# A filter layer and a feed-forward layer on one TensorE queue: stage 1 put well behind the transposing DMAs, groups placed anew, and the seven-product form from the third chunk on

## The chip, the cores and the metric

The kernel runs on one core of a Trainium2 chip. The time is the device time of one execution in microseconds (us). A profiled execution gives, beside its time, a trace of every instruction and DMA. Engines: PE is TensorE (PEld is its weight loading), DVE is VectorE, ACT is ScalarE, POOL is GpSimd, SP is SyncE, which here only starts DMAs. Each engine works through its own instructions in order.

## The reference

The reference filters a signal in the frequency domain and puts the result through a feed-forward layer:

```python
X = np.fft.rfft(x, axis=1)                      # x: 8 x 3008 x 256
y = np.fft.irfft(X * (filt_r + 1j * filt_i)[None], n=3008, axis=1)
h = y.reshape(24064, 256) @ w_in                # w_in: 256 x 2048
out = np.maximum(0.01 * h, h) @ w_out           # w_out: 2048 x 256
```

## The kernel before, in words

**The filter.** The FFT of 3008 = 94 x 32 points is done per batch entry in two steps, both as matmuls with constant matrices, then the multiplication, then the same two steps back. For batches 1 to 7 (batch 0 has a form of its own, at the head, from a list written out as text) there are four kinds of groups:

- stage 1 (`s1_group`, 16 groups per batch): four matmuls of 96 columns (L265) into one PSUM bank, and a copy (L266) by ScalarE, or by VectorE in some groups of batches 1 and 2, into the turn buffer `turn_in`.
- Six transposing DMAs (`t1_load`, L273) turn that buffer into six tiles `z1`. The buffer exists once: the copies of the next batch's stage 1 must wait until all six have read it.
- stage 2 (`s2_group`, 12 groups): two matmuls of 256 columns (L311); VectorE multiplies the bank with the filter (L320, L323); two DMAs exchange the halves of the partitions (L321, L322), except in every other group of batch 1, where VectorE writes the exchanged halves itself (L317, L318); GpSimd adds (L326).
- the first step back (`sa_group`): one matmul of 512 columns (L333), a ScalarE copy (L335), and after every second group a store to DRAM (L337). Eight loads (`t2_load`, L281) bring it back turned.
- the second step back (`sb_group`, 16 groups): four matmuls of 94 columns (L358) and copies (L347) into `yt`, the input of the feed-forward layer, a ring of six chunks.

**The feed-forward layer.** The 24064 rows go in 47 chunks of 512. For each chunk `moe1` does 32 matmuls of 512 columns (L524), and ScalarE takes each pair of results through the leaky ReLU (L527) into the chunk's tile. The second product is made one chunk later, in one of two forms:

- plain (`plain`): 4 x 16 matmuls of 256 columns (L689), a VectorE copy (L694) and a store for each of the four row tiles;
- seven products (`products`): seven products of 2 x 8 matmuls of 128 columns (L597), with four sums of activations made by VectorE ahead of them (`act_sums`, L563), one ScalarE copy (L637), and VectorE adds of the results (L625, L633, L641, L647, L650, L661). One of the seven is made a chunk later (`last_product`). Before the change chunks 0 to 2 are plain and chunks 3 to 46 have seven products (`W0 = 3`).

All results are stored through SyncE (L583), as are the transposing DMAs, the exchanges and the loads and stores of L281 and L337; loads of x go through GpSimd's queue (L204).

**The order.** Everything after the head is put in order by a planner that runs when the program is built. Its clock has 8 units for a chunk (some 15.3 us on the chip). Each chunk's matmuls have fixed places. Groups come from `PLANS`: for each batch the start and step of stage 1, start and step of stage 2, the lag of the first step back behind stage 2, start and step of the second step back, and start and step of the loads of x; batches above 4 repeat batch 4's row 47 units later. A group is taken at its time or at the first time at least `GAP` after the group before at which what it needs is due. `load_time` puts the transposing DMAs `TURN` behind the last stage-1 group and `TURNS` apart, and not more than `LEAD[0]` before stage 2 starts; stage 2 follows its DMA by `TURNED`. A stage-1 group of a batch above 1 is not taken earlier than `TURNS + 0.3` = 1.2 units behind the last transposing DMA of the batch before. `bank` gives a group the PSUM bank that the planner believes free first (a `hold` time per use). `AFTER`, `y_delay` and `SUMS` say how much later than its group, or than the chunk's start, an instruction is issued on its engine. These numbers set only the order on each engine; on the chip each instruction waits for what it needs by semaphores.

Of the kernel before, what the change touches and what calls it, by code (L numbers as in the profile page):

```python
# [19 lines left out]
N1, N2 = 94, 32  # L20
# [3 lines left out]
NW = 96  # L24
# [54 lines left out]
def kernel(  # L79
# [19 lines left out]
    SL = 8  # L99
    NCH = NCT // 2  # L100
    QT = 4 * N1
    W0 = 3
    GAP = 0.6
    EXG = 0
    LANDED = 2.43
    READ = 2.2
    TURN = 0.7
    TURNED = 2.2
    TURNS = 0.9
    SUMS = (0.09, 1.59, 2.35, 4)  # L110
    REST = (5.37, 14.61, 8.86, 10.48, 23.53, 20.72)
    DUE = (3.52, 0.66)
    TWICE = (2.2, 2.35)
    LEAD = (3.3, 7.37)
    AFTER = (0.53, 0.8, 1.33, 3.17, 0.39, 0.52)


    PLANS = (
        (0.68, 0.31, 12.6, 1.05, 4.3, 38.33, 2.78, 7.78, 1.5),
        (23.6, 0.8, 42.87, 2.62, 7.4, 85.59, 2.85, 7.0, 2.12),  # L120
        (46.5, 1.6, 77.28, 3.57, 5.62, 130.03, 2.65, 1.5, 2.2),
        (79.5, 2.2, 119.86, 3.87, 7.04, 177.42, 2.92, 1.5, 2.55),
    )

    f2_np, i1_np, small_np, i1t_np = _build_np_constants(N)
# [92 lines left out]

    EARLY = 6
    x_early = big[1][:].bitcast(FP32)[:, : EARLY * D].rearrange("p (n d) -> p n d", n=EARLY)  # L220
    nc.sync.dma_start(small_sb[:], small_d.ap())
    nc.sync.dma_start(x_early[:R1], bass.AP(tensor=x.tensor, offset=x.offset, ap=[[N2 * D, R1], [D, EARLY], [1, D]]))
    for n0, nn in ((6, 10), (16, 10), (26, 6)):
        x_load(0, n0, nn)
    for i in range(2):
# [32 lines left out]
    def s1_group(b, g, copy):  # L258
        h, dt = divmod(g, 2)

        def go():
            ps = bank("pf", 4, NW)
            need(("x", b, h if b > 1 else 0), *[("z1", b - 1, 5)] * (b > 1))
            for j in range(4):
                nc.tensor.matmul(ps[:, j, :], x_sb[:, 4 * h + j, ts(dt, P)], fwd1m[:, :NW], start=True, stop=True)  # L265
            copy(turn_in[:, :, dt, :, ds(4 * h, 4)], ps.rearrange("p n (q k) -> p k q n", q=4))  # L266
            issued.add(("s1", b, g))
        return go
# [31 lines left out]
    ys = {}  # L300

    def y_delay(b, g):
        return 1.2 if b == 1 and g % 2 == EXG else AFTER[2] if b > 1 else AFTER[3]

    def s2_group(b, g):
        def go():
            ps = bank("pf", 2, D, 1.75 if b == 1 and g % 2 == EXG else 1.2)
            need(("z1", b, g // 2))
            issued.add(("s2", b, g))
            for j in range(2):  # L310
                nc.tensor.matmul(ps[:, j, :], f2_sb[:, 2 * g + j, :],  # L311
                                 z1[g // 2][:, 2 * (g % 2) + j, :],
                                 start=True, stop=True)
            fa, fb = fa_sb[:, ds(2 * g, 2), :], fb_sb[:, ds(2 * g, 2), :]
            p1, p2, p3 = (scrp.tile([P, 2, D], FP32, tag=f"p{i}", name=f"p{i}_b{b}_g{g}") for i in (1, 2, 3))
            if b == 1 and g % 2 == EXG:
                nc.vector.tensor_tensor(p3[0:64], ps[64:P], fb[64:P], AL.mult)  # L317
                nc.vector.tensor_tensor(p3[64:P], ps[0:64], fb[0:64], AL.mult)  # L318
            else:
                nc.vector.tensor_tensor(p2[:], ps, fb, AL.mult)  # L320
                soon(AFTER[1], lambda: nc.sync.dma_start(p3[0:64], p2[64:P]))  # L321
                soon(AFTER[1], lambda: nc.sync.dma_start(p3[64:P], p2[0:64]))  # L322
            nc.vector.tensor_tensor(p1[:], ps, fa, AL.mult)  # L323
            ys[(b, g)] = y1 = ypp.tile([P, 2, D], FP16, tag="y", name=f"y_b{b}_g{g}")
            soon(y_delay(b, g), lambda: noted(
                ("y", b, g), lambda: nc.gpsimd.tensor_tensor(y1[:], p1[:], p3[:], AL.add)))  # L326
        return go
# [22 lines left out]
    def sb_group(b, g, copy):  # L350
        h, dt = g // 2, g % 2

        def go():
            ps = bank("pf", 4, NW)[:, :, :N1]
            need(("z2", b, h), ("i1t",))
            issued.add(("sb", b, g))
            for j in range(4):
                nc.tensor.matmul(ps[:, j, :], z2[h % 3][:, j, ts(dt, P)], i1_sb[:, 4 * h + j, :N1],  # L358
                                 start=True, stop=True)
            quad_copy(b, h, dt, ps, copy)  # L360
        return go
# [391 lines left out]
    while queue:  # L753
        time, n, stage, b, g, f = heapq.heappop(queue)
        t = max(time, last + GAP)
        if stage == 3:
            behind = when[2, b, g] + y_delay(b, g) + 0.02 if (2, b, g) in when else None
        else:
            behind = load_time(stage - 1, b, g // 2) if stage != 1 else 0
            if stage == 1 and b > 1:  # L760
                behind = load_time(1, b - 1, 5)
                behind = None if behind is None else behind + TURNS + 0.3
            if stage != 1 and behind is not None:
                behind += TURNED if stage == 2 else READ
        if behind is None or behind + 0.02 > t:
# [8 lines left out]
    for ci in range(NCHUNK + 1):  # L774
# [7 lines left out]
        for i, f in enumerate(items):  # L782
            at(SL * (ci + i / len(items)) + 0.01, f)
        if wino:
            for time, *what in [(v, i) for i, v in enumerate(SUMS)] if ci < NCHUNK else LAST:
                at(SL * ci + time, lambda ci=ci, what=what: act_sums(ci - 1, *what))
    while work:
        clock["now"], _, f = heapq.heappop(work)
# [31 lines left out]
```

## Time and profile before

| | us |
|---|---|
| three runs, median (lowest to highest) | 752.54 (751.26 to 752.71) |
| the profiled execution, its time | 753.01 |
| its span | 751.0 |
| TensorE busy | 734.5 |
| ScalarE busy | 549.2 |
| VectorE busy | 509.7 |
| GpSimd busy | 166.4 |

The span is the time from the first to the last instruction of the profiled execution; busy times are sums over instructions. Matmuls overlap in the array, so one of 512 columns shows 380 ns but the next can start 0.216 us after it. The head lasts until about 35.5 us, when the first matmul of the feed-forward layer starts; the last matmul starts at 746.4 us. "Granted clock" is the share of full speed at which TensorE's clock ran.

### The profile page before, as it was taken

The numbers are of one execution on the slowest core, as the hardware profiler recorded it, in microseconds if no ns is written. First come the engines' busy times: TensorE is split into PE (matmuls) and PEld (weight loads), VectorE is DVE, ScalarE is ACT, GpSimd is POOL, SyncE is SP. The second block draws the span as 40 slices with busy tenths as digits, with TensorE's granted clock in tenths as the row PEclk, the third lists the DMA queues.
The fourth block names the chain that finished last, engine by engine and source line by source line (L and its number), as shares of the span: only waits on it lengthen the run. The fifth ranks groups of instructions, "written<-read, shape, count | busy, mean of one in ns | idle before, by whom it ended". The sixth has DMA issues, their size and how long they took to land.

```text
span 751.0 us, 19526 instructions
## 1 busy us (share of the span) xinstructions
PE 734.5 (98%) x8129; PEld 523.9 (70%) x8129; DVE 509.7 (68%) x696; ACT 549.2 (73%) x763; POOL 166.4 (22%) x171
## 2 busy tenths in 40 slices
PE   8999998999899999999999999999999999999997
PEld 3566675776677777777777777777677777777776
DVE  7878556777566676677666767776577676556466
ACT  4775785787687877787788777877777777776762
POOL 5505401232222312222132331212122210000000
PEclk9999999999999999999999999999999999999999
DMA  9967758676856496465865558343664442212012
GB/s 206 222 106 166 186 127 168 145 177 141 186 135 145 120 176 159 116 146 128 166 150 135 134 140 185 99 130 100 122 174 117 109 111 90 63 54 65 29 46 69
DMA packets 128473, 98.44 MB, mean 131 GB/s; under 512 B 59152, under 2 KB 107152, under 8 KB 128192
## 3 DMA queue, kind: packets, MB, share of 16 engines
q1 hardware_dynamic: 113049, 79.51, 41.2%
q0 software_dynamic: 15056, 17.50, 15.9%
q8 instruction: 63, 1.03, 0.6%
q10 hardware_dynamic: 279, 0.19, 0.1%
q14 instruction: 26, 0.21, 0.1%
HBM read 45.97 MB, written 35.65 MB: 109 GB/s over the span
## 4 chain that ended last, share of the span: by engine, by line
PE 91%; DMA 4%; DVE 2%; ACT 1%; SPq 1%; issue 1%; POOL 0%; ACTq 0%; DVEq 0%; POOLq 0%
PE ph L524 42%; PE po_ps L597 18%; PE pf L597 18%; PE pf L265 3%; PE pf L311 2%; PE pf L333 2%; PE pf L358 2%; DMA big<-big 1%; PE pf L689 1%; PE po_ps L689 1%; DMA f_sb<-fwd_const 1%; DMA x_sb<-in_x_dram 1%; DVE big L563 1%; PE pf L432 0%; ACT yt L347 0%
## 5 line engine op out<-in xcount | busy, mean ns | idle before, releaser
L527 ACT ACTIVATE gt_c<-ph 128x1024 f16<-128x1024 f32 x376 | 384.9, 1024 | 133.0 <-PE ph L524 124.2
L524 PE MATMUL ph<-yt,w_in_sb 128*128 128x512 f16 x1504 | 448.8, 380 | 3.4 <-ACT gt_c L527 3.1
L597 PEld LDWEIGHTS <-gt_c 128*128 128x128 f16 x2800 | 201.7, 98 | 99.2 <-issue 1.7
L326 POOL TENSOR_TENSOR y_b_g<-p_b_g,p_b_g 128x512 f16<-128x512 f32 x84 | 116.8, 1392 | 437.1 <-DMA p_b_g<-p_b_g 292.8
L597 PEld LDWEIGHTS <-big 128*128 128x128 f16 x2128 | 151.6, 98 | 66.0 <-issue 0.5
L524 PEld LDWEIGHTS <-w_in_sb 128*128 128x128 f16 x1504 | 118.4, 98 | 9.2 <-issue 3.5
L320 DVE TENSOR_TENSOR p_b_g<-pf,fb_sb 128x512 f32<-128x512 f32 x78 | 53.6, 687 | 33.1 <-PE pf L311 23.5
L597 PE MATMUL po_ps<-wt_sb,gt_c 128*128 128x128 f16 x704 | 69.8, 219 | 0.0
L347 ACT CAST yt<-pf 128x376 f16<-128x376 f32 (+9 forms) x136 | 58.2, 441 | 14.7 <-PE pf L358 11.8
L597 PE MATMUL pf<-w_out_sb,gt_c 128*128 128x128 f16 x720 | 68.5, 221 | 0.0
L597 PE MATMUL pf<-wt_sb,gt_c 128*128 128x128 f16 x688 | 68.1, 219 | 0.0
L597 PE MATMUL pf<-wt_sb,big 128*128 128x128 f16 x704 | 67.9, 219 | 0.0
L597 PE MATMUL po_ps<-wt_sb,big 128*128 128x128 f16 x688 | 65.7, 219 | 0.0
L597 PE MATMUL po_ps<-w_out_sb,gt_c 128*128 128x128 f16 x688 | 65.0, 219 | 0.0
L563 DVE TENSOR_TENSOR big<-gt_c 128x2048 f16<-128x2048 f16 (+1 forms) x46 | 56.8, 1235 | 3.4 <-ACT gt_c L527 3.3
L563 DVE TENSOR_TENSOR big<-big,gt_c 128x2048 f16<-128x2048 f16 (+1 forms) x45 | 57.4, 1275 | 0.1
L323 DVE TENSOR_TENSOR p_b_g<-pf,fa_sb 128x512 f32<-128x512 f32 x84 | 57.2, 681 | 0.2
L563 DVE TENSOR_TENSOR big<-gt_c,big 128x2048 f16<-128x2048 f16 (+1 forms) x45 | 56.9, 1264 | 0.0
L563 DVE TENSOR_TENSOR gt_c<-gt_c 128x2048 f16<-128x2048 f16 x43 | 56.0, 1303 | 0.9
L335 ACT CAST big<-pf 128x512 f16<-128x512 f32 x84 | 49.0, 584 | 10.4 <-PE pf L333 8.2
L266 ACT CAST big<-pf 128x384 f16<-128x384 f32 x90 | 42.8, 476 | 16.5 <-DMA big<-big 8.1
L358 PE MATMUL pf<-i_sb,big 128*128 128x94 f16 x448 | 37.1, 207 | 0.0
(98 smaller groups left out, 644.9 us busy)
## 6 DMA issues: line engine op xcount, KB each, us to landing
p_b_g<-p_b_g SPq DMA_DIRECT2D x156, 128.0 KB
out_dram<-ost_c_h SPq DMA_DIRECT2D x118, 128.0 KB
dz<-big SPq DMA_DIRECT2D x42, 256.0 KB
big<-dz SPq DMA_DIRECT2D x56, 192.0 KB
x_sb<-in_x_dram POOLq DMA_DIRECT2D x40, 192.0 KB, 4.2
x_sb<-in_x_dram POOLq DMA_DIRECT2D x2, 768.0 KB, 8.8
w_in_sb<-in_moe_w_in_dram POOLq DMA_DIRECT2D x1, 1024.0 KB, 12.8
w_out_sb<-in_moe_w_out_dram POOLq DMA_DIRECT2D x1, 1024.0 KB, 13.7
```

The costliest lines, as they stand in the source:

```text
L265: nc.tensor.matmul(ps[:, j, :], x_sb[:, 4 * h + j, ts(dt, P)], fwd1m[:, :NW], start=True, stop=True)
L266: copy(turn_in[:, :, dt, :, ds(4 * h, 4)], ps.rearrange("p n (q k) -> p k q n", q=4))
L320: nc.vector.tensor_tensor(p2[:], ps, fb, AL.mult)
L323: nc.vector.tensor_tensor(p1[:], ps, fa, AL.mult)
L326: ("y", b, g), lambda: nc.gpsimd.tensor_tensor(y1[:], p1[:], p3[:], AL.add)))
L335: nc.scalar.copy(st2[h % 3][:, ds(2 * (g % 2), 2), :], ps)
L347: copy(yt[:, dt, ds(to, 4 * n)].rearrange("p (a c) -> p a c", c=4), v[:, ds(a, n)])
L358: nc.tensor.matmul(ps[:, j, :], z2[h % 3][:, j, ts(dt, P)], i1_sb[:, 4 * h + j, :N1], start=True, stop=True)
L524: nc.tensor.matmul(ph[:, j, :], w_in_sb[:, dt, ts(ct, P)], yt[:, dt, ds(ci * CH % RING, CH)], start=(dt == 0), stop=(dt == NDT - 1))
L527: nc.scalar.activation(gts[ci][:, ds(2 * g, 2), :], ph, AF.Lrelu)
L563: nc.vector.tensor_tensor(*(v[:, ds(c0, n)] for v in (o, i0, i1)), op)
L597: nc.tensor.matmul(of[t], a()[:, c, ts(t, P)], w[:, c, :], start=(c == 0), stop=(c == NCH - 1))
```

## The change

Three things change in what the program does, and many numbers of the planner change with them.

1. A stage-1 group may come no earlier than `MARGIN` = 3.069 units behind the last transposing DMA of the batch before (1.2 before). With the new `PLANS`, batch 3's first group stands at 47.4 (46.5), batch 4's at 81.5 (79.7), and the rows for batches 5 to 7 follow. `LEAD[0]` grows, so that the transposing DMAs stand 0.5 to 1 unit earlier. `TURN`, `TURNED`, `REST` and `AFTER` change by less.
2. `W0 = 2`: the third chunk (chunk 2) has seven products too. Its sums have places of their own, `SUMS_FIRST`; the sums of the others move a little.
3. The small constants are loaded in two DMAs instead of one, the first 128 columns ahead of the first rows of x and the rest behind them.

The bank's hold times and delays of `y_delay` become names in `YD`; of them 1.2 becomes 1.359 and 1.75 becomes 1.808.

```diff
-    W0 = 3
+    W0 = 2
...
-    TURN = 0.7
-    TURNED = 2.2
+    TURN = 1.257
+    TURNED = 2.062
     TURNS = 0.9
-    SUMS = (0.09, 1.59, 2.35, 4)
-    REST = (5.37, 14.61, 8.86, 10.48, 23.53, 20.72)
+    MARGIN = 3.069
+    YD = (1.359, 1.808, 1.2, 0.75, 1.163)
+    SUMS_FIRST = (0.01, 1.144, 2.226, 3.62)
+    SUMS = (0.322, 1.519, 2.723, 4)
+    REST = (5.579, 14.61, 8.86, 10.428, 23.53, 20.62)
     DUE = (3.52, 0.66)
     TWICE = (2.2, 2.35)
-    LEAD = (3.3, 7.37)
-    AFTER = (0.53, 0.8, 1.33, 3.17, 0.39, 0.52)
+    LEAD = (3.9, 7.37)
+    AFTER = (0.53, 0.689, 1.261, 3.17, 0.39, 0.52)
...
     PLANS = (
-        (0.68, 0.31, 12.6, 1.05, 4.3, 38.33, 2.78, 7.78, 1.5),
-        (23.6, 0.8, 42.87, 2.62, 7.4, 85.59, 2.85, 7.0, 2.12),
-        (46.5, 1.6, 77.28, 3.57, 5.62, 130.03, 2.65, 1.5, 2.2),
-        (79.5, 2.2, 119.86, 3.87, 7.04, 177.42, 2.92, 1.5, 2.55),
+        (0.68, 0.333, 12.656, 1.055, 4.3, 38.33, 2.78, 7.78, 1.457),
+        (23.6, 0.8, 42.87, 2.596, 7.146, 85.174, 3.056, 7.0, 2.022),
+        (47.4, 1.5, 76.756, 3.366, 5.62, 130.659, 2.634, 1.5, 1.552),
+        (81.5, 2.0, 119.86, 3.87, 7.04, 178.164, 2.92, 1.414, 2.55),
     )
...
-    nc.sync.dma_start(small_sb[:], small_d.ap())
+    nc.sync.dma_start(small_sb[:, 0], small_d.ap()[:, 0])
     nc.sync.dma_start(x_early[:R1], bass.AP(tensor=x.tensor, offset=x.offset, ap=[[N2 * D, R1], [D, EARLY], [1, D]]))
+    nc.sync.dma_start(small_sb[:, 1:], small_d.ap()[:, 1:])
...
     def y_delay(b, g):
-        return 1.2 if b == 1 and g % 2 == EXG else AFTER[2] if b > 1 else AFTER[3]
+        return YD[0] if b == 1 and g % 2 == EXG else AFTER[2] if b > 1 else AFTER[3]
...
-            ps = bank("pf", 2, D, 1.75 if b == 1 and g % 2 == EXG else 1.2)
+            ps = bank("pf", 2, D, YD[1] if b == 1 and g % 2 == EXG else YD[2])
...
             if stage == 1 and b > 1:
                 behind = load_time(1, b - 1, 5)
-                behind = None if behind is None else behind + TURNS + 0.3
+                behind = None if behind is None else behind + MARGIN
...
-            for time, *what in [(v, i) for i, v in enumerate(SUMS)] if ci < NCHUNK else LAST:
+            for time, *what in [(v, i) for i, v in enumerate(SUMS if ci - 1 > W0 else SUMS_FIRST)] if ci < NCHUNK else LAST:
```

## The prediction

> **What bounds the kernel now.** I read the page's busy shares and chain first, then the stretches of time with the granted clock, then what TensorE and ScalarE did in the two bad stretches, and last the SyncE queue there.
>
> The page says TensorE is the bound and holds almost the whole chain:
>
> ```profile
> PE 734.5 (98%) x8129; PEld 523.9 (70%) x8129; DVE 509.7 (68%) x696; ACT 549.2 (73%) x763; POOL 166.4 (22%) x171
> PE 91%; DMA 4%; DVE 2%; ACT 1%; SPq 1%; issue 1%; POOL 0%; ACTq 0%; DVEq 0%; POOLq 0%
> ```
>
> So only two things shorten the run: fewer TensorE columns, or less idle and less slow-clock time on TensorE. The view by stretches (columns: stretch, length, busy time of PE, PEld, DVE, ACT, POOL with counts, granted clock, DMA share, GB/s) shows where TensorE loses time. From 225 us to 525 us it is busy 25.00 of every 25 us but once (24.89). The loss is here:
>
> ```profile
> 75.00:100.00 25.00, 24.52 (x203) 16.77 (x201) 11.88 (x20) 18.32 (x25) 9.22 (x11) 1.00 0.84 187
> 125.00:130.00 5.00, 1.85 (x24) 1.26 (x22) 0.69 (x1) 2.32 (x3) 2.08 (x3) 1.00 0.80 156
> 130.00:135.00 5.00, 5.00 (x40) 3.47 (x38) 4.35 (x4) 2.90 (x5) 1.42 (x2) 0.66 0.84 171
> 195.00:200.00 5.00, 2.30 (x17) 1.43 (x16) 1.81 (x3) 1.78 (x3) 0.71 (x1) 0.85 0.98 222
> 200.00:205.00 5.00, 5.00 (x48) 3.57 (x47) 3.20 (x4) 3.15 (x5) 1.04 (x2) 0.80 0.71 151
> ```
>
> Each hole is followed by a slow stretch. The timelines of ScalarE and TensorE give the cause (last column: idle time before, and who ended it):
>
> ```profile
> 127.64 0.48 ACT L266 CAST big<-pf 128x384 f16<-128x384 f32 x1 [4.70 <-DMA big<-big]
> 129.10 0.59 PE L524 MATMUL ph<-yt,w_in_sb 128*128 128x512 f16 x2 [3.15 <-ACT gt_c L527]
> 197.89 0.48 ACT L266 CAST big<-pf 128x384 f16<-128x384 f32 x1 [3.43 <-DMA big<-big]
> 198.42 0.50 PE L311 MATMUL pf<-big,f_sb 128*128 128x256 f16 x2 [2.70 <-ACT big L266]
> ```
>
> L266 is the copy of a stage-1 group into the turn buffer. It must wait until the six transposing DMAs of the batch before have read that buffer. ScalarE works in order, so the leaky-ReLU evictions (L527) and other copies queue behind it, PSUM fills, and TensorE stops. The transposes are late because of their queue (SyncE's timeline):
>
> ```profile
> 111.10 1.28 SPq L273 DMA_TRANSPOSE big<-big x1
> 112.90 2.40 SPq L583 DMA_DIRECT2D out_dram<-ost_c_h  x3
> 115.34 4.05 SPq L273 DMA_TRANSPOSE big<-big  x3
> 119.50 1.22 SPq L583 DMA_DIRECT2D out_dram<-ost_c_h  x2
> 120.77 1.32 SPq L273 DMA_TRANSPOSE big<-big  x1
> 122.20 0.53 SPq L321 DMA_DIRECT2D p_b_g<-p_b_g  x1
> 122.77 0.60 SPq L322 DMA_DIRECT2D p_b_g<-p_b_g  x1
> 123.42 2.26 SPq L273 DMA_TRANSPOSE big<-big  x1
> ```
>
> Six transposes cost about 1.3 us each to issue, with stores (L583) and exchanges (L321, L322) between them; the last starts at 123.42 and lands 4.09 us later (3.10 us in the other case, by the chain).
>
> **The change part by part.**
>
> *Margin and plans.* I add the TensorE work between two points of each kernel's order (intervals from the timelines: 0.216 us for a 512-column matmul, 0.109 for 256, 0.056 for 128, 0.042 for 94 to 96). From the planned last transpose of batch 2 to the first stage-1 group of batch 3 there were 4.0 us of work; now 6.5. For batches 3 and 4: 2.5, now 7.2. Later batches have 14 to 15 instead of 9, and never waited. Batch 4's wait of 3.43 us meets 4.7 us of extra distance: it goes. Batch 3's wait of 4.70 meets 2.5 us: were the queue as late as before, 2.2 us would remain on ScalarE, and since 4.70 there cost TensorE 3.15, some 0.65 us on TensorE. But in the new SyncE order the second transpose is ahead of the three stores and the fifth ahead of the next two; adding the issue times above, the sixth starts some 2.8 us earlier against the TensorE work and lands about when the copy is due. Bounds 0 and 0.65; I take 0.3. Removed: 3.15 + 2.70 = 5.85 us of idling.
>
> *The slow clock.* Granted 0.66 over 5 us loses 1.70; 0.85 and 0.80 over 5 us each lose 0.75 and 1.00. Together 3.45 us. They follow the two holes and occur nowhere else between 25 us and 725 us; shorter holes (0.69 us in 170 to 175 us) left the clock at 1.00. With the holes gone I take all 3.45.
>
> [...]
>
> *Seven products from the third chunk.* Plain: 4 x 16 = 64 matmuls of 256 columns, 64 x 0.109 = 6.98 us. Seven products: 7 x 16 = 112 of 128 columns, 112 x 0.056 = 6.27 us. These two intervals are read here (four in 0.43 us; seven in 0.39 us):
>
> ```profile
> 52.64 0.60 PE L689 MATMUL pf<-w_out_sb,gt_c 128*128 128x256 f16 x4
> 53.07 0.59 PE L524 MATMUL ph<-yt,w_in_sb 128*128 128x512 f16 x2
> 119.09 0.55 PE L597 MATMUL pf<-wt_sb,gt_c 128*128 128x128 f16 x7
> 119.48 0.59 PE L524 MATMUL ph<-yt,w_in_sb 128*128 128x512 f16 x2
> ```
>
> That saves 0.71 us, all on the path. It adds VectorE work to a stage that had little: 4 sums of 1.22 to 1.30 us (L563), four adds of 0.42 and two of 0.69 us, less four plain copies of 0.42; ScalarE gets one copy of 0.38 (L637). On VectorE the first sum (plan time 24.01) waits for the last ReLU of the chunk and stands ahead of the filter products of batch 1's group 10 (24.08: 0.69 + 0.68 + 0.69 us). Group 10's bank is taken again by group 11 after 2.5 us of TensorE work (interval 43.4 to 46.1 of the running sum); the sum and the three products end at 46.9, so 0.8 us short. The parity of the product banks changes too: the first product now takes the bank that the last plain tile has just filled, and waits for its copy (0.31 us to its start, 0.42 long), 0.2 us. And the first stage-1 group of batch 2 takes the bank of the pair before it, whose copy (L335) stands behind a ReLU, 0.7 us; that wait is there now as well. They overlap, since each delays the next: about 1.0 us in all, against 0.48 us idle between 75 and 100 us now. Lower bound of the difference -0.5 (everything hidden), upper +1.5 (all three in a row, less today's loss); I take +0.3. Later sums also move (0.09 to 0.32, 2.35 to 2.72 of a chunk's 8): the nearest use is the fifth product at 4.57, still 3.5 us later (1.85 of 8, at 15.3 us a chunk), so nothing.
>
> *Order on SyncE at the later batches.* For batches 5, 6 and 7 the sixth transpose now stands ahead of the first pair of exchanges (L321, L322) instead of behind it, and batch 7's first transpose ahead of the exchange before it. Behind the exchange waits the GpSimd add (L326) and the first group of the next stage (L333). From the timelines, L326 ended 3.1, 1.9 and 0.05 us before L333 in these three. A transpose costs 1.25 to 2.51 us of queue; L333 is also planned up to 0.8 us earlier. Batch 5: no stall. Batch 6: 0.2 to 1.4. Batch 7: up to 2.5, less the 0.4 us by which batch 7's first transpose held up L311 and the 0.2 by which L333 waited for GpSimd, which both should go. In batch 7 the transposes that took 2.31 and 2.51 us were those just behind an exchange or a store, so in a row they may cost less. Bounds -0.6 and +3.5; I take +0.3, near the low end because the queue's total work is unchanged.
>
> *Head.* The small constants are loaded in two parts, with x's first rows between. ScalarE's first copy waited 3.64 us for those rows (until 5.88 us), and 128 KB fewer are ahead of them. But the stage goes on to wait for x_sb at 12.50 us and for f_sb at 20.07 us, loads of the GpSimd queue whose bytes are the same. Bounds -0.4 and +0.2 (one more transfer, 0.4 us to issue); I take 0. In the main loop batch 1's first transpose gets a store of 0.68 us ahead of it, and its user L311 is planned 0.8 us later: 0. The loads of x for batch 4 are spread over fewer us and end before batch 3's transposes start; they are used much later: 0.
>
> *Small VectorE coincidences.* The other short holes (0.69 us at 172, and tenths elsewhere) come from filter products behind a sum; the groups are placed anew, so some go and some come: 0, bounds -0.8 and +0.8.
>
> Sum: -5.85 - 3.45 - 0.71 + 0.3 + 0.3 + 0.3 = -9.1 us. The profiled execution took 753.01 us (span 751.0); that gives 743.9. The median of the runs is 0.47 lower, so **743.4 us**.
>
> **Rivals.**
>
> 1. *One long hole stays or a new one opens, with its slow stretch.* Likeliest places: batch 3's copy, or batch 7's first L333. For it: SyncE ran 2.5 to 4.3 us behind its plan at nearly every set of transposes. Against: the distances above. A hole of 2.7 us plus 1.7 of slow clock gives 747.8; with the other bounds up to 749.5.
>
> 2. *The slow clock is not due to the holes* and stays: 743.4 + 3.45 = 746.9. Against it stands that both slow stretches begin within a microsecond or two of a hole's end.
>
> 3. *Slower: the exchange behind the transposes.* At batches 5, 6 and 7 the first L333 waits for the add that waits for the exchange behind six transposes in a row. If each of the three holes reaches 2.7 us, each brings 1.7 us of slow clock: 3 x 4.4 = 13.2, 756.6 us. It decides from about 1.4 us at each, if holes that short already slow the clock (3 x 3.1 = 9.3); no row shows that (0.69 us did not, 2.70 did). For it: L326 already ends only 0.05 us early in batch 7. Against: batch 5 has 3.1 us to give.
>
> 4. *No change:* the copies wait as before, because the transposes wait for something planned with them (the last stage-1 copy, now 2.5 to 2.7 us of work ahead at batches 2 and 3, 3.6 and 4.3 before). Then only 0.7 us is won: 751.8 and, with the coincidences, anything around 752.
>
> **How the numbers follow.** Forecast 0.74; rival 1 0.11; rival 2 0.03; rival 3 0.08; rival 4 0.04. The forecast's own terms give 740.9 (all lower bounds) to 747; rival 1 reaches 749.5. Leaving out rivals 3 and 4 and the last tenths below, the range is 741.0 to 749.5. A difference under 0.2% (1.5 us) can't be told from none here. Faster: forecast, rivals 1 and 2, 0.88; the same 0.04; slower 0.08.
>
> **What the changed kernel's profile would show.** ScalarE's L266 no longer waits on the transposing DMA for more than about a microsecond; the granted clock is 1.00 in all stretches of 25 us; TensorE's busy time between 100 and 225 us is 24.5 or more of each 25. L689 falls from 192 to 128 matmuls, L597 grows by 112. Idle of about 1 us around 79 to 84 us, before L311 and L265. At batches 6 and 7 a wait of L333 on L326 of up to 2 us. The prediction is wrong if a hole over 2.5 us appears anywhere in the main loop, or if L266 still waits several microseconds.

## The result and the profile after

| | before | after |
|---|---|---|
| median of five executions each (lowest to highest; three of the five before are those of the table above) | 751.26 us (750.27 to 752.71) | 742.57 us (742.34 to 743.89) |
| ratio, with its 95% interval | | 0.9887 [0.9868, 0.9905] |
| the profiled execution: time, span | 753.01, 751.0 | 743.38, 741.6 |

The change is worth 1.1%. In the kernel after, the lines of `products` and of the groups stand 3 or 4 lines lower: L269 and L270 are stage 1's matmul and copy (L265 and L266 before), L277 the transposes, L285 the loads of `z2`, L325 and L326 the exchanges, L330 GpSimd's add, L337 the first step back, L362 the second, L528 and L531 the first product and its ReLU, L601 the seven products.

The page after, busy times and chain:

```profile
PE 731.5 (99%) x8177; PEld 521.9 (70%) x8177; DVE 515.0 (69%) x702; ACT 549.1 (74%) x764; POOL 170.2 (23%) x171
PE 90%; DMA 4%; POOL 2%; DVE 1%; ACT 1%; issue 1%; SPq 0%; POOLq 0%; DVEq 0%; ACTq 0%
```

TensorE's 8177 matmuls are 48 more than before: 64 plain ones of the third chunk went and 112 of its seven products came. The view by stretches of the kernel after (columns as before):

```profile
75.00:100.00 25.00, 24.20 (x250) 16.55 (x248) 19.43 (x27) 19.17 (x28) 10.11 (x11) 1.00 0.81 180
125.00:150.00 25.00, 24.66 (x286) 17.93 (x284) 19.80 (x25) 20.39 (x31) 10.75 (x13) 1.00 0.84 184
175.00:200.00 25.00, 24.43 (x279) 17.57 (x277) 18.20 (x25) 19.46 (x30) 6.25 (x5) 1.00 0.88 191
525.00:550.00 25.00, 24.81 (x274) 17.72 (x273) 16.53 (x24) 17.92 (x23) 5.12 (x4) 1.00 0.78 174
```

The two stretches with holes of several microseconds have less than 0.6 us idle each, and the granted clock is 1.00 everywhere in the main loop. What is left can be seen in the timelines of ScalarE and TensorE of the kernel after (last column: idle time before, and who ended it):

```profile
126.15 0.48 ACT L270 CAST big<-pf 128x384 f16<-128x384 f32 x1 [1.98 <-PE pf L315]
192.13 0.48 ACT L270 CAST big<-pf 128x384 f16<-128x384 f32 x1 [1.12 <-DMA big<-big]
...
83.08 0.33 PE L269 MATMUL pf<-small_sb,x_sb 128*128 128x96 f16 x4 [0.50 <-ACT big L339]
127.61 0.59 PE L528 MATMUL ph<-yt,w_in_sb 128*128 128x512 f16 x2 [0.26 <-ACT gt_c L531]
197.77 0.34 PE L362 MATMUL pf<-i_sb,big 128*128 128x94 f16 x4 [0.56 <-DMA big<-dz]
277.47 0.38 PE L337 MATMUL pf<-y_b_g,small_sb 128*128 128x512 f16 x1 [0.45 <-POOL y_b_g L330]
453.65 0.38 PE L337 MATMUL pf<-y_b_g,small_sb 128*128 128x512 f16 x1 [0.37 <-POOL y_b_g L330]
541.92 0.38 PE L337 MATMUL pf<-y_b_g,small_sb 128*128 128x512 f16 x1 [0.19 <-POOL y_b_g L330]
```

The first copies of batches 3 and 4 (126.15, 192.13) waited 4.70 and 3.43 us before, now 1.98 and 1.12. The view puts the first of the two down to a matmul, but it was the transposes as well: the trace's record of DMA completions has the sixth transpose, started at 122.34, complete at 126.01, 0.14 us before the copy starts; before, the same two times were 127.50 and 127.64. TensorE's idle time now lies in small waits such as these six, and three of them are for GpSimd's add behind the exchanges. The SyncE queue before batch 3's copy shows the new order, with the second transpose ahead of the three stores and the fifth ahead of the next two:

```profile
108.45 1.29 SPq L277 DMA_TRANSPOSE big<-big  x1
110.08 0.31 SPq L285 DMA_DIRECT2D big<-dz  x1
110.44 1.25 SPq L277 DMA_TRANSPOSE big<-big  x1
112.21 2.44 SPq L587 DMA_DIRECT2D out_dram<-ost_c_h  x3
114.69 4.09 SPq L277 DMA_TRANSPOSE big<-big  x3
118.89 2.12 SPq L587 DMA_DIRECT2D out_dram<-ost_c_h  x2
121.12 0.54 SPq L325 DMA_DIRECT2D p_b_g<-p_b_g  x1
121.70 0.59 SPq L326 DMA_DIRECT2D p_b_g<-p_b_g  x1
122.34 1.39 SPq L277 DMA_TRANSPOSE big<-big  x1
```

To compare executions I take a *hole* as the distance between the starts of two matmuls that follow each other in the main loop, less the interval of the first (0.216 us for 512 columns, 0.109 for 256, 0.056 for 128, 0.042 for 94 to 96, as in the prediction). Work is the sum of these intervals, so it is counted and not measured. The two profiled executions, from the first instruction to the end:

| us | before | after | difference |
|---|---|---|---|
| head, until the first L524 (L528) | 35.53 | 34.88 | -0.65 |
| work: the sum of the intervals | 697.8 | 697.1 | -0.7 |
| holes and slow clock | 13.07 | 5.06 | -8.0 |
| from the last matmul's start to the end | 6.59 | 6.34 | -0.25 |
| the execution | 753.01 | 743.38 | -9.6 |

### The profile page after: what moved, and what is told of

Same layout as the page of the kernel before. It is cut to its first block, busy times and chain, and to the rows that moved or that the text cites. A ratio compares the mean times of both kernels' runs of the same rounds, so it can differ in the third digit from the quotient of the medians.

```text
span 741.6 us, 19629 instructions
## 1 busy us (share of the span) xinstructions
PE 731.5 (99%) x8177; PEld 521.9 (70%) x8177; DVE 515.0 (69%) x702; ACT 549.1 (74%) x764; POOL 170.2 (23%) x171
## 4 chain that ended last, share of the span: by engine, by line
PE 90%; DMA 4%; POOL 2%; DVE 1%; ACT 1%; issue 1%; SPq 0%; POOLq 0%; DVEq 0%; ACTq 0%
PE ph L528 42%; PE pf L601 18%; PE po_ps L601 18%; PE pf L362 2%; PE pf L337 2%; PE pf L315 2%; PE pf L269 2%; DMA fa_sb<-in_filt_r_dram 1%; DMA p_b_g<-p_b_g 1%; DMA fa_sb<-in_filt_i_dram 1%; POOL y_b_g L330 1%; PE po_ps L693 1%; PE pf L693 1%; POOL prod L416 0%; ACT yt L351 0%
## 5 line engine op out<-in xcount | busy, mean ns | idle before, releaser
L531 ACT ACTIVATE gt_c<-ph 128x1024 f16<-128x1024 f32 x376 | 385.3, 1025 | 131.9 <-PE ph L528 122.5
L528 PE MATMUL ph<-yt,w_in_sb 128*128 128x512 f16 x1504 | 447.3, 379 | 0.4 <-ACT gt_c L531 0.3
L601 PEld LDWEIGHTS <-gt_c 128*128 128x128 f16 x2864 | 206.1, 98 | 101.0 <-issue 0.7
L330 POOL TENSOR_TENSOR y_b_g<-p_b_g,p_b_g 128x512 f16<-128x512 f32 x84 | 120.4, 1434 | 424.2 <-DMA p_b_g<-p_b_g 299.3
L601 PEld LDWEIGHTS <-big 128*128 128x128 f16 x2176 | 154.3, 98 | 68.5 <-issue 1.1
L528 PEld LDWEIGHTS <-w_in_sb 128*128 128x128 f16 x1504 | 117.2, 98 | 6.0 <-issue 0.6
L601 PE MATMUL pf<-wt_sb,gt_c 128*128 128x128 f16 x720 | 71.2, 219 | 0.0
L601 PE MATMUL po_ps<-wt_sb,gt_c 128*128 128x128 f16 x704 | 71.0, 219 | 0.0
L601 PE MATMUL po_ps<-w_out_sb,gt_c 128*128 128x128 f16 x752 | 70.4, 219 | 0.1
L601 PE MATMUL pf<-wt_sb,big 128*128 128x128 f16 x720 | 68.8, 219 | 0.0
L601 PE MATMUL po_ps<-wt_sb,big 128*128 128x128 f16 x704 | 68.4, 219 | 0.0
L601 PE MATMUL pf<-w_out_sb,gt_c 128*128 128x128 f16 x688 | 65.0, 219 | 0.0
L567 DVE TENSOR_TENSOR big<-gt_c 128x2048 f16<-128x2048 f16 (+1 forms) x47 | 59.8, 1272 | 0.3 <-ACT gt_c L531 0.2
L270 ACT CAST big<-pf 128x384 f16<-128x384 f32 x90 | 42.9, 477 | 12.1 <-PE pf L269 7.8
L362 PE MATMUL pf<-i_sb,big 128*128 128x94 f16 x448 | 37.0, 206 | 0.6 <-DMA big<-dz 0.6
```

Source lines behind the costliest of these rows:

```text
L528: nc.tensor.matmul(ph[:, j, :], w_in_sb[:, dt, ts(ct, P)], yt[:, dt, ds(ci * CH % RING, CH)], start=(dt == 0), stop=(dt == NDT - 1))
L531: nc.scalar.activation(gts[ci][:, ds(2 * g, 2), :], ph, AF.Lrelu)
L567: nc.vector.tensor_tensor(*(v[:, ds(c0, n)] for v in (o, i0, i1)), op)
L601: nc.tensor.matmul(of[t], a()[:, c, ts(t, P)], w[:, c, :], start=(c == 0), stop=(c == NCH - 1))
```

## The experiments

The theory: TensorE's idle time came from stage-1 copies that waited for late transposes; distance takes the wait away, the slow clock goes with the holes, and the third chunk adds its own 0.7 us. The rivals: a new wait takes the place of the old (the exchange behind a row of transposes); the slow clock has another cause; the gain comes from another part of the change. Kernels told of together ran side by side on one chip with the kernel before.

**The margin alone.** The kernel before, with one number changed:

```diff
-                behind = None if behind is None else behind + TURNS + 0.3
+                behind = None if behind is None else behind + 3.069
```

> The kernel before with one number changed: a stage-1 group may come no earlier than 3.069 units (not 1.2) behind the last transposing DMA of the batch before. All else as before: plans, transposes, third chunk plain. Batch 3's first group moves from 46.5 to 47.17 and batch 4's from 79.71 to 81.58. Theory 1 (the holes are stage-1 copies waiting for the transposing DMAs, and the slow clock follows a hole): batch 4's hole goes with its slow clock (-2.7, -1.75 us); batch 3's copy still waits 4.7 - 1.3 = 3.4 us, and TensorE stands 3.15 - 1.3 = about 1.9 us. If a hole of 1.9 us slows the clock, the time is the kernel before's less 5.8 us, about 745.5; if not, less 7.5 us, about 743.8. Theory 2 (the gain of the change lies elsewhere: the third chunk, the order of SyncE): no change, about 751. [...]

Measured: 747.79 us (745.28 to 750.90, 7 executions) against 751.23 (747.12 to 753.20, 18); ratio 0.9952 [0.9934, 0.9970]. That is less than half of the gain. In its profile the first copy of batch 4 waits 0.88 us (3.43 before) and that of batch 3 still 2.60 (4.70 before), as ScalarE's timeline has it:

```profile
127.33 0.48 ACT L266 CAST big<-pf 128x384 f16<-128x384 f32 x1 [2.60 <-PE ph L524]
```

The view names a matmul here too, but the last transpose completed at 127.19, 0.14 us before this copy. In place of the hole of 3.31 us behind it there are two of 0.55 and 0.49 us; the larger loss is another, which its timelines of SyncE, GpSimd and TensorE show at batch 3's first step back:

```profile
184.15 7.53 SPq L273 DMA_TRANSPOSE big<-big  x5
191.79 1.72 SPq L321 DMA_DIRECT2D p_b_g<-p_b_g  x1
193.56 0.58 SPq L322 DMA_DIRECT2D p_b_g<-p_b_g  x1
...
196.41 1.26 POOL L326 TENSOR_TENSOR y_b_g<-p_b_g,p_b_g 128x512 f16<-128x512 f32 x1 [11.21 <-DMA p_b_g<-p_b_g]
...
197.73 0.38 PE L333 MATMUL pf<-y_b_g,small_sb 128*128 128x512 f16 x1 [2.16 <-POOL y_b_g L326]
```

Five transposes in a row take 7.53 us of SyncE's queue; the exchange behind them starts at 191.79, the add at 196.41, and L333 stops TensorE in a hole of 2.32 us. This is the prediction's third rival (the exchange behind the transposes), at batch 3 instead of batches 5 to 7. The row of five stands in the kernel before as well:

```profile
188.34 7.64 SPq L273 DMA_TRANSPOSE big<-big  x5
```

There TensorE had already stopped for the copy of batch 4 (the hole of 2.87 us until 198.42), so nothing was seen of it. The margin shortens one wait, and what is queued behind the transposes becomes the next; with the new `PLANS`, where exchanges stand between the transposes (at 187.63 and 188.22 us, ahead of the sixth, in the kernel after), its hole is 0.99 us or less in the profiles of the kernel after.

**Stage 1 put back, third chunk alone plain, small constants in one DMA.** Three kernels, each the kernel after with one part undone:

```diff
# stage 1 back (the loads of x keep their places)
-    MARGIN = 3.069
+    MARGIN = 1.2
-        (47.4, 1.5, 76.756, 3.366, 5.62, 130.659, 2.634, 1.5, 1.552),
-        (81.5, 2.0, 119.86, 3.87, 7.04, 178.164, 2.92, 1.414, 2.55),
+        (46.5, 1.5, 76.756, 3.366, 5.62, 130.659, 2.634, 2.4, 1.552),
+        (79.7, 2.0, 119.86, 3.87, 7.04, 178.164, 2.92, 3.214, 2.55),
# third chunk plain
-    W0 = 2
+    W0 = 3
# small constants in one DMA
-    nc.sync.dma_start(small_sb[:, 0], small_d.ap()[:, 0])
+    nc.sync.dma_start(small_sb[:], small_d.ap())
-    nc.sync.dma_start(small_sb[:, 1:], small_d.ap()[:, 1:])
```

With the new starts `MARGIN` itself binds nothing: the same order comes out with 1.2 and with 3.069, so it was not tried apart from them.

> The changed kernel with stage 1 put back alone: MARGIN 1.2, batch 3's stage 1 from 46.5 and batch 4's from 79.7 (loads of x kept at their places). Transposes, third chunk and the rest as changed. Theory 1: batch 3's copy is due about 1.0 to 1.8 us before the transposes land, which costs TensorE 0 to 0.3 us, since the transposes start earlier than in the kernel before; batch 4's copy waits about 3.3 us again and TensorE stands about 2.7 us, with a slow stretch of 1.7 us behind: 742.6 + 4.4 = 747.0, and 745.3 if the clock holds. Theory 2: as the changed kernel, 742.6.

> The changed kernel with W0 = 3: the third chunk plain again, stage 1 and plans as changed. Theory 1: 0.71 us more matmul time, 0.4 to 0.8 us less idle between 79 and 91 us (the wait for the product bank, 0.25, goes; those for VectorE and ScalarE shrink): 742.4 to 743.0, not to be told from the changed kernel by time; in the trace TensorE's idle time after the third chunk's start falls by that much. Theory 2 (the third chunk carries the gain): several us slower, 747 or more.

> The changed kernel with the small constants loaded in one DMA ahead of x, as before. If the split shortened the head, the first matmul of the feed-forward layer comes at about 35.5 us again instead of 34.9 and the time grows by 0.65 us to 743.2. If the head differs from run to run by that much, it comes anywhere between 34.8 and 35.6 and the time stays at 742.6.

| | us (lowest to highest) | ratio to before |
|---|---|---|
| stage 1 back | 748.70 (745.99 to 751.48, 12 executions) | 0.9968 [0.9948, 0.9987] |
| third chunk plain | 746.09 (743.53 to 748.40, 6) | 0.9930 [0.9908, 0.9951] |
| small constants in one | 743.61 (743.25 to 745.31, 4) | 0.9900 [0.9884, 0.9916] |

Stage 1 put back brings both holes back, as the timelines of ScalarE and TensorE show:

```profile
127.03 0.48 ACT L270 CAST big<-pf 128x384 f16<-128x384 f32 x1 [3.90 <-DMA big<-big]
195.86 0.48 ACT L270 CAST big<-pf 128x384 f16<-128x384 f32 x1 [2.91 <-DMA big<-big]
...
128.49 1.01 PE L528 MATMUL ph<-yt,w_in_sb 128*128 128x512 f16 x2 [2.18 <-ACT gt_c L531]
196.39 0.38 PE L315 MATMUL pf<-big,f_sb 128*128 128x256 f16 x2 [2.18 <-ACT big L270]
```

Holes of 2.35 and 2.34 us, each followed by 3.41 us at half clock in this execution (750.34 us). Three of its twelve executions had a granted clock of 1.000 and took 745.99 to 746.69 us; the four at 0.994 and 0.995 took 750.04 to 751.48. So without the half clock the holes cost some 3.4 to 4.1 us against the kernel after (its median of 742.57, from another set of runs), and the executions with it take about 4 us more, of which two windows of 1.71 are 3.41. I had expected less of a wait at batch 3, since the new order of transposes stays. The wait of 3.90 us, 0.8 less than before, shows what this order does for batch 3's copy; the distance does the rest, from 3.90 to 1.98 and at batch 4 from 2.91 to 1.12.

The third chunk plain, 0.7 us by its columns, gives back 2.5 us by the medians (746.09 against the 743.61 of the kernel with only its constants undone; the two intervals overlap). Where they come from the profiles don't show. Here are ScalarE's copies of batches 3 and 4 with the third chunk plain, and behind them those with the constants in one DMA (that kernel is a line shorter, so L269 is its L270):

```profile
127.02 0.48 ACT L270 CAST big<-pf 128x384 f16<-128x384 f32 x1 [2.29 <-DMA big<-big]
193.91 0.48 ACT L270 CAST big<-pf 128x384 f16<-128x384 f32 x1 [1.99 <-DMA big<-big]
...
127.59 0.48 ACT L269 CAST big<-pf 128x384 f16<-128x384 f32 x1 [2.20 <-DMA big<-big]
193.75 0.48 ACT L269 CAST big<-pf 128x384 f16<-128x384 f32 x1 [1.41 <-DMA big<-big]
```

The first waits are alike, the second 0.6 us apart, and the holes of the whole main loop sum to 5.41 and 5.60 us. The profiled execution of the plain form (745.00 us) is one of its faster three; it spreads over 4.9 us, with two of the six executions at a clock of 0.998. My expectation allowed for the columns and the handover only and missed; the cause is open. The small constants are worth nothing that these runs can tell from none: the interval holds the kernel after's ratio.

**The kernel after again, with more distance, and with all its small waits treated.** Side by side:

```diff
# more distance (the third chunk plain in a second form: W0 = 3)
+        (48.2, 1.5, 76.756, 3.366, 5.62, 130.659, 2.634, 2.2, 1.552),
+        (82.6, 2.0, 119.86, 3.87, 7.04, 178.164, 2.92, 1.414, 2.55),
# smoothed: stage 1 later by less, first step back later from batch 4 on,
# batch 2's second step back later, the other product bank first in plain
+        (23.6, 0.8, 42.87, 2.596, 7.146, 85.9, 3.056, 7.0, 2.022),
+        (47.8, 1.5, 76.756, 3.366, 5.62, 130.659, 2.634, 3.0, 1.552),
+        (82.1, 2.0, 119.86, 3.87, 7.5, 178.164, 2.92, 1.414, 2.55),
-            po = out_banks[(done["products"] + tj) % 2].rearrange("p a t d -> p (a t d)")[:, :D]
+            po = out_banks[(done["products"] + tj + 1) % 2].rearrange("p a t d -> p (a t d)")[:, :D]
```

> The changed kernel itself, beside the next three on one chip. Its margins at batches 3 and 4 are thin (ScalarE still waited 1.1 us for the transposing DMAs at batch 4 in its profile), so a DMA queue that runs a microsecond later costs it tenths: 742.3 to 744.5.

> The changed kernel with stage 1 still further behind the transposes: batch 3 from 48.2 instead of 47.4, batch 4 from 82.6 instead of 81.5 (9.1 and 8.6 us of TensorE work behind the last transpose instead of 6.5 and 7.2). Theory 1 (what is left at batches 3 and 4 is the same wait): ScalarE no longer waits for the transposing DMAs there, the 0.4 us of idle at 127 us goes, the runs lie closer together, median 742.0 to 742.8. Theory 2 (the rest is not that wait): as the changed kernel. The load of batch 2's turned data is 0.8 us nearer to its use, so the 0.7 us of idle at 197 us may grow to 1.5.

> The same with W0 = 3, the third chunk plain. With the third chunk plain and the distances of the changed kernel the median was 746.1, with runs from 743.5 to 748.4, although its matmuls are only 0.71 us longer. If that came from the thin distances at batches 3 and 4 (a hole in some executions), then with more distance the plain form costs 0 to 0.7 us against the run before and its runs lie as close together: 742.0 to 743.5. If the third chunk's form itself is worth 3 us or more, this is 745 or more.

> The changed kernel with its remaining short holes attacked: the plain chunks take the other of the two product banks (0.25 us at 80 us), batch 2's last stage starts at 85.9 instead of 85.2 (0.73 at 197), the first step back follows stage 2 by 7.5 instead of 7.04 units from batch 4 on (0.61, 0.53, 0.36 at 277, 453, 542), stage 1 of batches 3 and 4 from 47.8 and 82.1. If each hole goes and none opens, 2.0 us less: 740.5; if groups placed anew open others, 741 to 743.

| | us (lowest to highest) | ratio to before (751.31, 11 executions) |
|---|---|---|
| the kernel after | 743.36 (742.46 to 744.23, 6) | 0.9901 [0.9881, 0.9921] |
| more distance | 743.15 (742.83 to 745.57, 6) | 0.9906 [0.9883, 0.9928] |
| more distance, third chunk plain | 744.71 (743.60 to 747.99, 6) | 0.9924 [0.9900, 0.9949] |
| smoothed | 741.44 (740.77 to 742.35, 6) | 0.9877 [0.9857, 0.9896] |

With more distance no copy waits for the transposes in the profile and the hole of 0.43 us at 127 us is gone, but the time is the same. The longest hole is now the one for the exchange at batch 3; its TensorE timeline:

```profile
193.06 0.38 PE L337 MATMUL pf<-y_b_g,small_sb 128*128 128x512 f16 x1 [0.99 <-POOL y_b_g L330]
```

That hole is 1.15 us, and 1.38 in the plain form. It stands in this group's execution of the kernel after as well (0.99), though not in the first profile of that kernel: one profiled execution does not show every hole. So the change's distance is enough. The plain form still spreads more widely (743.6 to 748.0), against what I expected. In its profile no copy waits for the transposes either, but that is an execution of 743.81 us, which shows no hole long enough for 748; why the plain third chunk makes it spread stays open.

The smoothed version treats the waits the profile of after showed, and all its six executions lie below all six of the kernel after. Its holes and slow clock sum to 2.82 us (5.06 after); two of the stretches:

```profile
125.00:150.00 25.00, 25.00 (x291) 18.31 (x290) 21.03 (x27) 20.15 (x32) 9.18 (x11) 1.00 0.78 170
525.00:550.00 25.00, 25.00 (x279) 17.95 (x277) 16.42 (x23) 18.74 (x25) 5.80 (x4) 1.00 0.75 167
```

It is the best version of this study.

**Batch 3's first step back later, and the third chunk alone.** The lag of batch 3's first step back was raised in the kernel after and in the smoothed one, and the third chunk's form was put into the kernel before by itself:

```diff
# batch 3's lag in the kernel after; the same number in the smoothed one
-        (47.4, 1.5, 76.756, 3.366, 5.62, 130.659, 2.634, 1.5, 1.552),
+        (47.4, 1.5, 76.756, 3.366, 6.4, 130.659, 2.634, 1.5, 1.552),
# third chunk alone, in the kernel before
-    W0 = 3
+    W0 = 2
+    SUMS_FIRST = (0.01, 1.144, 2.226, 3.62)
-            for time, *what in [(v, i) for i, v in enumerate(SUMS)] if ci < NCHUNK else LAST:
+            for time, *what in [(v, i) for i, v in enumerate(SUMS if ci - 1 > W0 else SUMS_FIRST)] if ci < NCHUNK else LAST:
```

> The changed kernel with one number changed: batch 3's first step back follows its stage 2 by 6.4 units instead of 5.62 (11.8 instead of 10.3 us of TensorE work for the first group). Theory 1: what is left at 192 us is the wait of L333 for the GpSimd add behind the exchange behind the transposes (0.99 us in the last profile of the changed kernel); it goes, unless another appears, and the time falls by up to 1 us: 742.4, from 743.4. Theory 2 (the wait has another cause, such as the filter bank): it stays at about 1 us and the time at 743.4.

> The smoothed kernel (other product bank for the plain chunks, batch 2's last stage later, lag 7.5 from batch 4 on, stage 1 of batches 3 and 4 from 47.8 and 82.1) with batch 3's lag at 6.4 as well. The 0.34 us left at 192 us goes: 741.1, from 741.4.

> The kernel before with the third chunk in seven products and its sums at the new places, and nothing else. Theory 1: 0.71 us less matmul time and 0.3 to 0.8 us more idle around 80 to 90 us, the two holes as before: 750.5 to 751.5, not to be told from the kernel before. Theory 2 (the third chunk's form carries 3 us): 748 or less.

| | us (lowest to highest) | ratio to before (749.92, 17 executions) |
|---|---|---|
| after, batch 3's lag 6.4 | 743.17 (742.17 to 744.33, 6) | 0.9898 [0.9871, 0.9925] |
| smoothed, batch 3's lag 6.4 | 742.08 (741.51 to 742.43, 5) | 0.9884 [0.9852, 0.9916] |
| before, third chunk alone | 752.16 (750.46 to 754.54, 12) | 1.0025 [1.0006, 1.0044] |

With the longer lag the hole before batch 3's first L337 is gone in both, and nothing is won. The first has holes of 0.70 us at 127 and at 168 us and 0.41 at 194; the order of its matmuls differs from the kernel after's only from 192 us on, so the first two are the execution's own, as are 0.43 us at 127 us and 0.64 at 128 us in two executions with the unchanged order. The second has one of 1.43 us, where L362 waits for its load behind the same queue. TensorE's timelines, of the first and of the second:

```profile
168.49 0.39 PE L337 MATMUL pf<-y_b_g,small_sb 128*128 128x512 f16 x1 [0.54 <-DVE p_b_g L327]
```

```profile
198.14 0.34 PE L362 MATMUL pf<-i_sb,big 128*128 128x94 f16 x4 [1.27 <-DMA big<-dz]
```

The third chunk alone is no gain but a small loss (the interval leaves 0.06% to 0.44%), though its work sums to 697.1 us, 0.7 less, as it should. The ScalarE and TensorE timelines of that kernel (one line lower than in before):

```profile
195.37 0.48 ACT L267 CAST big<-pf 128x384 f16<-128x384 f32 x1 [4.57 <-DMA big<-big]
...
127.96 0.59 PE L525 MATMUL ph<-yt,w_in_sb 128*128 128x512 f16 x2 [2.75 <-ACT gt_c L528]
195.90 0.59 PE L312 MATMUL pf<-big,f_sb 128*128 128x256 f16 x2 [3.84 <-ACT big L267]
```

Batch 4's copy waits longer (4.57 us, 3.43 before), its hole is 4.00 us (2.87), and two windows at half clock follow it. All twelve executions have a granted clock of 0.995 or less; of the 46 executions of the kernel before in these three groups 24 do. So a part that saves 0.7 us of columns lost more than that, and in the profile the loss stands in a stage over 100 us later.

**Holes of chosen lengths.** Which hole brings the half clock? The first results contradicted each other: 2.35 us did, 2.32 us did not. A kernel with holes made on purpose: the kernel after, with extra ReLU evictions of the same bank in fourteen chunks, five to ten halves each, which repeat work and hold TensorE up.

```diff
+    HOLES = {10: 5, 12: 6, 16: 7, 18: 8, 22: 9, 24: 10, 28: 5, 30: 6, 34: 7, 36: 8, 38: 9, 40: 6, 42: 7, 44: 8}
...
+        if ct == 9:
+            for n in [2] * (HOLES.get(ci, 0) // 2) + [1] * (HOLES.get(ci, 0) % 2):
+                nc.scalar.activation(gts[ci][:, ds(2 * g, n), :], ph[:, :n], AF.Lrelu)
```

> The changed kernel with holes of known places: in 14 chunks between the 10th and the 44th, ScalarE repeats the eviction of the fifth pair (1.02 us whole, 0.58 us half) 2.5 to 5 times before the real one, so that TensorE runs out of free PSUM and stands for about 1 to 3.5 us. The matmuls are those of the changed kernel. Theory 1: the slow clock follows some of the holes of 2 us and more and none of the short ones; the lengths at which it does are what is asked. [...]

Measured: 794.86 us (794.42 to 800.22, 4 executions). Holes of 2.44, 2.70, 3.03, 3.75, 3.92 and 4.13 us were followed by the half clock; holes of 2.02, 2.07, 2.13, 2.24, 2.70, 3.12, 3.29 and 3.29 were not. Length alone decided nothing: one of 2.70 was and another was not. What decided shows when the starts of the half-clock stretches are set side by side: 394.87, 429.00, 527.99, 592.84, 657.70, 719.14, 790.82. Their distances are 10, 29, 19, 19, 18 and 21 times 3.413 us, each to within 0.01 us; in the profile of before, 130.28 and 198.54 are 20 times 3.413 apart, and its trace has either stretch as 3.413 us long. In these traces, then, the half-clock stretches lie on a fixed grid of windows of 3.413 us. Here is the view by stretches on that grid, three places of the kernel with the holes (second number after the stretch: TensorE busy; the number before the last two: granted clock):

```profile
295.89:299.30 3.41, 1.46 (x16) 0.98 (x16) 0.00 (x0) 3.35 (x7) 1.26 (x1) 1.00 0.28 78
299.30:302.71 3.41, 3.41 (x42) 2.56 (x41) 1.36 (x3) 3.03 (x5) 0.00 (x0) 1.00 0.00 0
...
524.58:527.99 3.41, 1.13 (x15) 0.77 (x13) 1.89 (x3) 3.35 (x5) 0.00 (x0) 1.00 0.29 65
527.99:531.40 3.41, 3.41 (x25) 2.29 (x24) 0.00 (x0) 1.66 (x3) 1.26 (x1) 0.50 0.30 72
...
620.15:623.56 3.41, 1.98 (x25) 1.39 (x22) 1.95 (x3) 3.31 (x4) 0.83 (x1) 1.00 0.56 137
623.56:626.97 3.41, 1.71 (x19) 1.23 (x19) 0.00 (x0) 3.17 (x5) 0.43 (x1) 1.00 0.02 5
626.97:630.38 3.41, 3.41 (x38) 2.35 (x36) 1.49 (x3) 2.63 (x4) 0.00 (x0) 1.00 0.26 77
```

and the two holes of the kernel before:

```profile
126.86:130.28 3.42, 1.18 (x14) 0.85 (x14) 0.28 (x1) 2.59 (x4) 1.90 (x3) 1.00 0.82 157
130.28:133.69 3.41, 3.41 (x23) 2.41 (x22) 3.41 (x4) 1.60 (x3) 1.14 (x2) 0.50 0.88 172
195.13:198.54 3.41, 0.71 (x10) 0.48 (x8) 0.69 (x1) 0.65 (x2) 0.00 (x0) 1.00 0.98 197
198.54:201.96 3.42, 3.42 (x22) 2.26 (x21) 2.63 (x3) 1.95 (x4) 1.75 (x2) 0.50 0.68 165
```

The hole of 2.44 us (at 525.4) lies inside one window, leaves it 1.13 us busy, and the next window runs at half clock. The hole of 3.29 (at 622.0) is split between two windows, 1.98 and 1.71 us busy, and nothing happens. In the 14 profiled executions of this study, the drain at the end of the program included (it gives the grid where nothing else does), 25 full-clock windows with 1.37 us busy or less were each followed by one at half clock (14 of them in a drain), and 16 with 1.45 to 2.15 us busy were not (4 in a drain). A window of half clock cost 1.71 us, half of its 3.413, where TensorE had work throughout. Where the half-clock window itself was busy for only 1.73 and 1.86 us, the next was at half clock too; those busy for 3.09 or more ended it.

## Why the prediction was right

The forecast of 743.4 us stands against 742.57, and for the profiled execution 743.9 against 743.38. By its steps:

| step | predicted | measured |
|---|---|---|
| holes at batches 3 and 4 | 5.85 removed, 0.3 left | holes of 3.31 and 2.87 gone, 0.43 left at batch 3 |
| slow clock | -3.45 | two windows of 1.71: -3.41 |
| columns of the third chunk | -0.71 | -0.7 |
| its handover, 75 to 100 us | +0.3 | idle 0.48 to 0.80: +0.32 |
| exchanges at batches 5 to 7 | +0.3 | 0.53 at batch 6, 0.36 at batch 7; before, 0.55 (L311) and 0.36 (L333) at batch 7: 0 |
| head | 0 | -0.65 in this pair |
| small coincidences | 0 | 0.85 at 172 us and 0.27 at 416 gone; 0.61 at batch 4's L337 and 0.73 at batch 2's L362 new: +0.2 |
| the end, behind the last matmul | 0 | -0.25 in this pair |

The rows on holes and slow clock sum to -8.6 us where the table of the two executions has -8.0; by subtraction the other 0.6 is in holes of less than 0.4 us that no row names. That the profiled execution came out within half a microsecond of the sum is luck in part: these 0.6 us lost stand against 0.9 won at the head and the end, and no step held either. The bounds of the terms add up to 740.2 and 749.2 us, not to 740.9 and 747 as the prediction has it; the stated range holds the result all the same. Not every sign came as told: TensorE was busy for 24.43 us between 175 and 200 us, where 24.5 was the least foretold.

*Margin and plans.* The mechanism is shown: put back, both waits return; distance alone in the kernel before brings them down to 2.60 and 0.88 us. Some details were off. I called batch 4's wait gone, and 1.12 us of it remained on ScalarE without stopping TensorE; "no more than about a microsecond" of wait was too low for batch 3 (1.98). At batch 3 the sixth transpose was to start 2.8 us earlier. Counted from the first matmul of the main loop it started 0.4 us earlier (87.46 us, 87.89 before) and landed 0.8 earlier (91.13, 91.97): two stores of 2.12 us together and a pair of exchanges still stand ahead of it. So the wait was close to the 2.2 us that I gave for a queue as late as before; the 0.43 us on TensorE lie within the bounds 0 and 0.65, but that I took 0.3 rested on a start that did not come. And I argued this step as distance against lateness of the copies, while the margin alone, which gives part of that distance (batch 3's first group at 47.17 instead of 47.4, the transposes no earlier), won 3.4 us only. The queue's order from the new `PLANS` is a part of it too: without it the exchange behind five transposes opens a hole of 2.32 us. Rival 3 was the right danger at the wrong batch.

*The slow clock.* Removed as predicted, and rival 2 falls: every half-clock window in the traces follows a window with a hole. In the 14 profiles it was enough that TensorE was idle for about 2.0 us (3.41 less 1.37 to 1.45) within one window of the grid. So the 3.45 us were not a fixed cost of the kernel before but that of an execution in which both holes fell badly. Taking the grid's position as arbitrary, which is an assumption, an idle time h between 2.0 and 4.0 us would bring a window of half clock with a chance of 1 - (4.0 - h)/3.41: by this estimate, from those windows alone, 0.75 and 0.62 for the 3.15 and 2.70 us of the two holes (idle time as the timelines have it, 0.16 to 0.17 less than the holes as counted here), 1.37 windows per execution. By their granted clock, some 24 of 46 executions of the kernel before had two (751.8 us on average), 18 had one (749.6) and 4 none (748.0): 1.43. The steps are 2.2 and 1.6 us, beside the 1.71 of one window. This accounts for a part of the wide spread of the kernel before (within the 24 some 3 us are left, 750.4 to 753.7) and fits the narrow one of the kernel after, whose holes are all under 1 us.

*Seven products.* The columns and the handover are as predicted (0.25 us for the product bank, 0.66 for batch 2's first stage-1 group; I had 0.2 and 0.7; group 11's bank brought no hole of its own, and the work ahead of it, 43.4 to 46.1, is 2.7 us and not 2.5). By its own figures, 1.0 less 0.48, the term should have been +0.5 and not the +0.3 that came. What no step of mine held is that this part acts on the rest: undone, it costs 2.5 us by the medians instead of 0.4 (1.6 with more distance); alone, it gains nothing. That the terms could simply be added was an assumption, and it held for the whole change without holding for its parts: the change without the third chunk's form -5.1 us (746.09 against 751.23), that form alone +2.2 (752.16 against 749.92), both together -7.6 in the first set (743.61, constants in one DMA) and -8.7 in the runs of the result.

*SyncE at later batches.* Batch 5 has no stall, as predicted; batches 6 and 7 are at the low end, and the wait at batch 4, which I had not costed, is the largest of this kind in the profile (0.61 us). Nor had I costed batch 3's, of 0.98 to 0.99 us in three later profiles with the same order up to there. Likewise batch 2's second step back, whose load now stands behind three stores and two exchanges (0.73 us).

*Head.* The 0.65 us between the two profiled executions is not shown to be the split: the main loop starts between 34.57 us (third chunk alone, without the split) and 35.71 (stage 1 back, with it) in 13 profiled executions, and at 36.19 in the fourteenth, that of the kernel after with the constants in one DMA. The means, 35.01 us over ten profiles with the split and 35.46 over four without, lean to its side, but four executions with the constants in one DMA have nearly the kernel after's time. So 0 within what can be told.

## What to carry to other kernels

An in-order DMA queue that feeds several engines is a balance: moving one consumer away from late transfers only helps if what is queued behind these transfers (the exchanges in this kernel) does not become the next late one (with the margin alone it did, in a hole of 2.32 us), so read the queue's order after the move and look for long runs of one kind. In these runs a hole in TensorE's work cost its own length and, where about 2 us of idle time (2.04 or more in 25 of 25) fell into one window of 3.413 us, a further 1.71 us, with a chance that by the estimate above grows with the length (0.62 for 2.70 us, 0.75 for 3.15). Many small holes were better than a few long ones: the kernel after, with holes all under 1 us, kept a clock of 1.00 throughout the main loop. A kernel whose executions spread by a few microseconds (here 748.0, 749.6 and 751.8 us on average with no, one and two such windows) is worth searching for such holes. Do not add the gains of parts that share a queue without trying them alone: here 0.7 us of saved columns was worth nothing without the other part and 1.6 to 2.5 us with it, and why is open.

## What was not expected of the hardware

- In the 14 profiles the clock fell by windows of a fixed grid of 3.413 us. A full-clock window of 1.37 us busy or less was followed by one at half clock (25 of 25), one of 1.45 or more was not (16 of 16 between 1.45 and 2.15). Two holes of the same 2.70 us differed, and one of 3.29 did nothing where one of 2.44 did.
- Five transposes in a row took 7.53 us of SyncE's queue, 1.51 each, and three took 4.09 and 4.70. In the 14 profiles the 302 transposes that stand right behind another took 1.34 us each at the median, the 286 others 1.32, and both kinds have some of 2 us and more. In a row they were not cheaper, as the prediction thought possible; the two of 2.31 and 2.51 us in batch 7 took 1.30 and 1.26 in the kernel after, one behind a store and one in a row.
- Open: why the plain third chunk makes the executions spread (743.5 to 748.4 us), also with more distance; and why, with the third chunk's form changed alone in the kernel before, the copy of batch 4 waits longer for the transposes over 100 us later.
